# A reworked start: tile-wise gate steps, a fourth step in spare PSUM banks, and one transposing DMA per tile

## The chip, the cores and the metric

The kernel runs on one core of one Trainium2 chip. The metric is the device time of one execution in microseconds; 185.24 us is the median of three runs of the kernel before the change (185.03 to 185.57).

## What is computed

The input x is 2048 rows of 448. Each row is normalised; the normalised rows feed a gated network and a complex linear recurrence, and the two results are multiplied and added to x:

```
xn = layernorm(x)                                   # 2048 x 448
h[t] = Lam_bar * h[t-1] + B_bar @ xn[t]             # complex, 448 states
s = 2 * real(h @ C) + xn * Dskip
g = silu((sigmoid(xn @ w_gate) * (xn @ w_up)) @ w_down)     # inner width 1792
out = x + s * g
```

## The kernel before

**Tiling.** The 2048 rows are four chunks of 512, a chunk is four tiles of 128 rows. A chunk needs its normalised rows transposed: `xnT` holds seven slots of 512 columns. In slot s the partitions 0 to 63 hold features 64s to 64s+63 and the partitions 64 to 127 the next 64 features, round the end of the 448. TensorE uses it in two halves: lines 707 and 708 issue a pair of matmuls with 64 contracted rows each, one on the lower and one on the upper half of the array, and the two run beside each other. A step (`gu_step`) is one block m of 128 gate or up columns in both halves of the inner width: seven such pairs over the 512 columns of a chunk, into one of three two-bank PSUM tiles `gu`. `g0.3` is gate block 3 of chunk 0, `u0.0` up block 0. The gate result leaves PSUM through a Tanh on ScalarE (line 721), the up result through VectorE (line 724). Two further one-bank PSUM tiles, `acc`, are used in turn by the transposes, by `b_phase` and by the output matmuls.

**The head.** Chunk 0 is started by hand (lines 962 to 989). TensorE first runs matmuls on zeros (L418). The tiles 0 to 3 of x are loaded on the SP and ACT queues, the gate weights in three blocks for each half of the width (m 0 to 1, 2 to 3, 4 to 6), the lower half on SP and the upper on ACT. A tile goes through `stats` (L424, L425, VectorE), the square root on ScalarE (L450), a reciprocal (L452) and the normalisation (L469, VectorE). `pe_transpose` (L501 to 503) transposes it with eight TensorE operations, six over the full array and two of 64 columns, into an `acc` bank, and a copy brings it to `xnT` (tile 0 on ScalarE, L506; the others on VectorE, L509). `columns` (L540, L542) turns three small parameter rows into columns. The gate steps m 0 and 1 then take tiles 0 and 1 one at a time; after the transposes of tiles 2 and 3 come m 2 over two tiles, then m 0, 1 and 2 over tiles 2 and 3, and then the ordinary steps from `g0.3`.

**Later chunks.** `norm` runs on ScalarE (L474), POOL copies the first 64 features to the end of the 512-wide row buffer `xn` (L477), and `dma_transpose` issues two transposing DMAs a tile on SP (L375): one for the even slots and one for the odd. `skip_row` (L482) multiplies the same buffer by `dbc`, the broadcast Dskip. There are eight `xn` buffers.

**Order.** TensorE's order is that of the program text, VectorE's too while `pl.seq` is set. Everything else is ordered by a list scheduler (`Plan`) from the costs and transfer rates written in the code; it fixes the order before the run, and at run time each engine keeps it and waits for what it needs. DMAs issued on SP and ACT share eight completion semaphores in turn, so that the ninth waits for the landing of the first, and so on. SP issues in this order: x tile 0, three gate blocks, two up blocks (one for each half), x tiles 4 to 7 as one transfer, two up blocks, `dbc`, the B matrices (L375), the transposes of chunk 1.

Of the kernel before, what the change touches and what calls it, by code (L numbers as in the profile page):

```python
# [18 lines left out]
D = 448  # L19
F = 1792  # L20
P = 128
# [224 lines left out]
def kernel(  # L246
# [39 lines left out]
    NXN = 8  # L286
    xn = [sbt(f"xn{i}", [512]) for i in range(NXN)]
    xnT_raw = [sbt(f"xnT{i}", [7 * L]) for i in range(3)]
    xnT = [flat(t[:], 7, L) for t in xnT_raw]
    hF_raw = [sbt(f"hF{i}", [FT * L]) for i in range(2)]  # L290
# [69 lines left out]
    BLK = {"g": [(0, 2), (2, 4), (4, 7)], "u": [(0, 3), (3, 7)]}  # L360
# [25 lines left out]
    load_w("SP", "g", 0, 0, rate=90e3)  # L386
    load_w("SP", "g", 0, 1)
    load_x(1, 1, "ACT")
    load_x(2, 2, "ACT")
    load_w("ACT", "g", 1, 0, rate=90e3)  # L390
    load_w("SP", "g", 0, 2)
    load_w("ACT", "g", 1, 1)
    load_w("ACT", "g", 1, 2)
# [13 lines left out]
    for h in range(2):  # L407
        load_w("SP", "u", h, 0, rate=215e3)
    load_x(4, 4, rate=140e3)
    for h in range(2):  # L410
        load_w("SP", "u", h, 1, rate=260e3)
    load("SP", "dbc", P * D * 2, dbc[:], A_Dskip.unsqueeze(0).to_broadcast((P, D)))
# [53 lines left out]
    def norm(t):  # L466
        b = t % NXN
        if t < TPC:
            add("DVE", 0.42, lambda: V.tensor_scalar(out=xn[b][:, 0:448], in0=x_all[:, t, :],  # L469
                                                     scalar1=meanf[:, t, :], scalar2=rsd[:, t, :],  # L470
                                                     op0=ALU.subtract, op1=ALU.mult),
                r=[("x", t), ("mf", t), ("rs", t)], w=[("xn", b)])
        else:
# [3 lines left out]
            add("POOL", 0.2, lambda: G.tensor_copy(out=xn[b][:, 448:512], in_=xn[b][:, 0:64]),  # L477
# [6 lines left out]

    acc_n = [0]
# [9 lines left out]
    def pe_transpose(t):  # L495
        b, a, js = t % NXN, next_acc(), slice(t * P, t * P + P)
        tp = flat(acc[a][:].bitcast(BF16)[:, 0:7 * P], 7, P)

        def f():
            for s in range(6):  # L500
                T.transpose(tp[:, s, :], xn[b][:, s * H:s * H + P], ident[:, :])  # L501
            T.transpose(tp[0:H, 6, :], xn[b][:, 384:448], ident[:, :])
            T.transpose(tp[H:P, 6, :], xn[b][:, 0:H], ident[:, :])
        add("PE", 0.46, f, r=[("xn", b), "ident"], w=[("acc", a)])
        if t == 0:
# [6 lines left out]
    def dma_transpose(t):  # L512
        b, c = t % NXN, t // TPC
        js = slice((t % TPC) * P, (t % TPC) * P + P)
        k = ("xnT", c % 3, t % TPC)
        al = ["xnT2free"] if c == 2 else []
        tload([k + ("a",)], xnT[c % 3][:, 0:7:2, js], xn[b][:], P * 1024, r=[("xn", b), ("xnw", b)] + al)
        tload([k + ("b",)], xnT[c % 3][:, 1:6:2, js], xn[b][:, 64:448], P * 768, r=[("xn", b)] + al)
# [16 lines left out]
    def columns(a):  # L535
        vps = flat(gu[a][:, 0, 0:12], 4, 3)
# [6 lines left out]
        add("PE", 0.4, f, r=["ident"] + [("vrow", k) for k in range(3)], w=[("gu", a)])  # L543
        pv = sbt("pv", [3, 4], FP32)
        dt_b = C("dt", 4, BF16)
        add("DVE", 0.1, lambda: V.tensor_copy(out=pv[:].rearrange("p k i -> p i k"), in_=vps[:]), r=[("gu", a)], w=["pv"])
# [150 lines left out]
    SW = 0.1  # L697

    def gu_mm(c, k, m, a, lo, hi, first):
        x = xnT[c % 3]  # L700
        ts = slice(lo * P, hi * P)
# [3 lines left out]
        def f():  # L705
            for s in range(7):
                T.matmul(gu[a][:, 0, ts], lhsT=w_[0:H, s, ms], rhs=x[0:H, s, ts], start=(s == 0), stop=(s == 6))  # L707
                T.matmul(gu[a][:, 1, ts], lhsT=w_[H:P, (s + 1) % 7, ms], rhs=x[H:P, s, ts],  # L708
# [3 lines left out]
                   r=xr(c, lo, hi) + [("w", k, 0, m), ("w", k, 1, m)], w=[("gu", a)], name=f"{k}{c}.{m}")  # L712
# [3 lines left out]
    def gu_evac(c, k, m, a):  # L716
# [3 lines left out]
        if k == "g":  # L720
            add("ACT", act(1024), lambda: A.activation(th, gu[a][:], ACT.Tanh, scale=0.5),  # L721
                r=[("gu", a)], w=[tk])
        else:
            add("DVE", dve1(1024), lambda: V.scalar_tensor_tensor(out=ho, in0=th, scalar=1.0, in1=gu[a][:],  # L724
                                                                 op0=ALU.add, op1=ALU.mult),
                r=[("gu", a), tk], w=[hk])
# [23 lines left out]
    def b_phase(c, mid=None):  # L750
# [5 lines left out]
        rs = [(slice(0, H), 6), (slice(H, P), 5)]  # L756
# [210 lines left out]
    for t in (0, 1):  # L967
        chain(t, 1)
        norm(t)
# [125 lines left out]
```

## Time and profile before

| what | value |
|---|---|
| median of the runs shown | 185.24 us |
| the profiled execution: span from the first to the last instruction | 183.7 us |
| difference, what lies around the span | about 1.5 us |
| TensorE's granted clock over the span | 1.000 |
| first full-array transpose, tile 0 | 5.34 us after the start of the span |
| first gate pair | 7.89 us |
| `g0.3` starts | 13.87 us |
| `u0.0` starts | 19.91 us |

The profiled execution has a span; its own full time is not listed apart from the three runs, so the 1.5 us is taken against their median.

The trace also gives, for each DMA, the time from its issue to its landing. For the transfers of the head, in order of landing (sizes in KB of 1024 bytes; the last column adds the sizes up):

| transfer | queue | issued at, us | landed at, us | KB | KB so far |
|---|---|---|---|---|---|
| x tile 0 | SP | 0.7 | 3.1 | 112 | 112 |
| x tile 1 | ACT | 0.8 | 3.4 | 112 | 224 |
| x tiles 2, 3 | ACT | 1.2 | 5.1 | 224 | 448 |
| gate, lower, m 0-1 | SP | 1.2 | 7.08 | 224 | 672 |
| gate, upper, m 0-1 | ACT | 1.7 | 7.54 | 224 | 896 |
| gate, lower, m 2-3 | SP | 2.0 | 9.09 | 224 | 1120 |
| gate, upper, m 2-3 | ACT | 2.4 | 9.80 | 224 | 1344 |
| gate, lower, m 4-6 | SP | 2.6 | 11.16 | 336 | 1680 |
| gate, upper, m 4-6 | ACT | 3.2 | 12.26 | 336 | 2016 |
| up, lower, m 0-2 | SP | 7.1 | 14.21 | 336 | 2352 |
| up, upper, m 0-2 | SP | 7.7 | 15.82 | 336 | 2688 |
| x tiles 4-7 | SP | 8.4 | 19.04 | 448 | 3136 |
| up, lower, m 3-6 | SP | 9.1 | 20.88 | 448 | 3584 |
| up, upper, m 3-6 | SP | 9.8 | 22.48 | 448 | 4032 |
| dbc | SP | 11.2 | 22.66 | 112 | 4144 |

How to read the profile: an engine's share of the span says nothing of what sets the end; the chain of waits does. A stretch in which an engine's busy time equals the stretch cannot be shortened by an earlier arrival of its data, only by less work or by starting it earlier. The landing of a transfer is later than its issue by the queue ahead of it, and here that queue is most of it.

### The profile page before, as it was taken

The numbers are of one execution on the slowest core, as the hardware profiler recorded it, in microseconds if no ns is written. First come the engines' busy times: TensorE is split into PE (matmuls) and PEld (weight loads), VectorE is DVE, ScalarE is ACT, GpSimd is POOL, SyncE is SP. The second block draws the span as 40 slices with busy tenths as digits, with TensorE's granted clock in tenths as the row PEclk, the third lists the DMA queues.
The fourth block names the chain that finished last, engine by engine and source line by source line (L and its number), as shares of the span: only waits on it lengthen the run. The fifth ranks groups of instructions, "written<-read, shape, count | busy, mean of one in ns | idle before, by whom it ended". The sixth has DMA issues, their size and how long they took to land.

```text
span 183.7 us, 3601 instructions
## 1 busy us (share of the span) xinstructions
PE 177.4 (97%) x1402; PEld 90.4 (49%) x1402; DVE 166.4 (91%) x296; ACT 94.8 (52%) x152; POOL 34.2 (19%) x95
## 2 busy tenths in 40 slices
PE   7699999999999999999999999999999999999992
PEld 2585555465554444455554444444555444455551
DVE  3873899899999998999999999999999998999973
ACT  3689993958599978665310452367120445211100
POOL 7370465000048557700000000000000000000000
PEclk9999999999999999999999999999999999999999
DMA  5999994489801370243000000002000000001121
GB/s 137 255 225 223 155 166 90 90 256 266 231 0 26 74 82 21 50 82 71 0 2 0 29 0 0 4 0 75 0 4 0 25 25 5 25 0 52 57 73 50
DMA packets 30258, 13.44 MB, mean 73 GB/s; under 512 B 19744, under 2 KB 30240, under 8 KB 30240
## 3 DMA queue, kind: packets, MB, share of 16 engines
q1 hardware_dynamic: 28336, 12.05, 30.7%
q10 hardware_dynamic: 1808, 1.15, 2.5%
q8 instruction: 11, 0.18, 0.4%
q14 instruction: 7, 0.06, 0.1%
q0 software_dynamic: 96, 0.00, 0.0%
HBM read 6.77 MB, written 1.84 MB: 47 GB/s over the span
## 4 chain that ended last, share of the span: by engine, by line
PE 93%; DMA 3%; DVE 1%; issue 1%; POOL 1%; DVEq 0%; POOLq 0%
PE gu L707 45%; PE gu L903 14%; PE acc L932 11%; PE acc L903 9%; PE gu L775 8%; DMA hF<-in_A_Lambda_re_dram 3%; PE gu L708 2%; PE acc L778 2%; PE gu L761 2%; POOL hF L353 1%; PE acc L501 0%; DVE o_t L948 0%; PE acc L764 0%; DVE o_t L944 0%; DVE o_t L941 0%
## 5 line engine op out<-in xcount | busy, mean ns | idle before, releaser
L708 PE MATMUL gu<-xnT,wG 64*128 64x512 bf16 (+2 forms) x245 | 46.0, 333 | 0.0
L707 PE MATMUL gu<-xnT,wG 64*128 64x512 bf16 (+2 forms) x245 | 46.0, 333 | 0.0
L707 PE MATMUL gu<-xnT,wU 64*128 64x512 bf16 x196 | 45.8, 376 | 0.0
L708 PE MATMUL gu<-xnT,wU 64*128 64x512 bf16 x196 | 45.8, 376 | 0.0
L721 ACT ACTIVATE sig<-gu 128x1024 f32<-128x1024 f32 x21 | 21.3, 1021 | 22.0 <-PE gu L708 21.9
L903 PEld LDWEIGHTS <-hF 128*128 128x128 bf16 x224 | 21.9, 98 | 20.7 <-issue 0.2
L707 PEld LDWEIGHTS <-wG 64*128 64x128 bf16 x245 | 21.9, 94 | 18.7
L707 PEld LDWEIGHTS <-wU 64*128 64x128 bf16 x196 | 18.4, 94 | 22.1
L724 DVE SCALAR_TENSOR_TENSOR hF<-sig,gu 128x1024 bf16<-128x1024 f32 x21 | 25.5, 1216 | 2.9 <-PE gu L708 1.6
L903 PE MATMUL gu<-wd,hF 128*128 128x448 bf16 x140 | 27.9, 352 | 0.0
L842 DVE TENSOR_TENSOR_SCAN wv<-c_r,st,z 128x512 bf16<-128x512 f32 x18 | 22.9, 1276 | 0.0
L932 PE MATMUL acc<-cT,hT 128*128 128x448 bf16 (+1 forms) x112 | 22.6, 346 | 0.0
L708 PEld LDWEIGHTS <-wG 64*128 64x128 bf16 x245 | 21.8, 94 | 0.0
L909 ACT ACTIVATE g_t<-gu 128x448 bf16<-128x448 f32 x10 | 5.4, 541 | 29.2 <-DVE o_t L946 12.9
L708 PEld LDWEIGHTS <-wU 64*128 64x128 bf16 x196 | 18.4, 94 | 0.0
L789 ACT CAST bus<-gu 128x1024 bf16<-128x1024 f32 x12 | 11.9, 1011 | 12.4 <-PE gu L761 12.2
L903 PE MATMUL acc<-wd,hF 128*128 128x448 bf16 x84 | 16.9, 352 | 0.0
L775 PE MATMUL gu<-xnT,bT 128*128 128x512 bf16 x72 | 16.7, 379 | 0.0
L932 PEld LDWEIGHTS <-hT 128*128 128x128 bf16 x119 | 11.5, 98 | 10.1 <-issue 0.4
L424 DVE BATCH_NORM_STATS2 bst<-x_all 128x6 f32<-128x448 bf16 x12 | 7.0, 610 | 5.7 <-DMA x_all<-in_A_x_dram 5.7
L795 ACT CAST bus<-acc 64x256 bf16<-64x256 f32 (+1 forms) x24 | 8.8, 369 | 6.4 <-PE acc L778 6.1
L944 DVE TENSOR_TENSOR o_t<-acc,xd 128x448 bf16<-128x448 f32 (+1 forms) x16 | 9.6, 601 | 1.3 <-PE acc L932 1.2
(138 smaller groups left out, 240.1 us busy)
## 6 DMA issues: line engine op xcount, KB each, us to landing
out_dram<-o_t SPq DMA_DIRECT2D x15, 112.0 KB, 1.7
wd<-in_B_w_down_dram SPq DMA_DIRECT2D x2, 784.0 KB, 5.5
x_all<-in_A_x_dram SPq DMA_DIRECT2D x3, 448.0 KB, 4.5
wU<-in_B_w_up_dram SPq DMA_DIRECT2D x2, 448.0 KB, 12.2
wU<-in_B_w_up_dram SPq DMA_DIRECT2D x2, 336.0 KB, 7.6
wG<-in_B_w_gate_dram SPq DMA_DIRECT2D x2, 224.0 KB, 6.5
wG<-in_B_w_gate_dram ACTq DMA_DIRECT2D x2, 224.0 KB, 6.6
xnT<-xn SPq DMA_TRANSPOSE x24, 2.4
```

The lines of the kernel that those rows point to most:

```text
L424: add("DVE", 0.6, lambda: V.bn_stats(out=bst[b][:], in_=x_all[:, t, :]), r=[("x", t)], w=[("bst", b)])
L707: T.matmul(gu[a][:, 0, ts], lhsT=w_[0:H, s, ms], rhs=x[0:H, s, ts], start=(s == 0), stop=(s == 6))
L708: T.matmul(gu[a][:, 1, ts], lhsT=w_[H:P, (s + 1) % 7, ms], rhs=x[H:P, s, ts], start=(s == 0), stop=(s == 6))
L721: add("ACT", act(1024), lambda: A.activation(th, gu[a][:], ACT.Tanh, scale=0.5), r=[("gu", a)], w=[tk])
L724: add("DVE", dve1(1024), lambda: V.scalar_tensor_tensor(out=ho, in0=th, scalar=1.0, in1=gu[a][:], op0=ALU.add, op1=ALU.mult), r=[("gu", a) ...
L775: T.matmul(gu[slots[pt]][:, i, :], lhsT=bT[:, kt, i, pt * P:pt * P + P], rhs=x[:, 2 * kt, :], start=(first and kt == 0), stop=(not first a ...
L789: add("ACT", act(1024), lambda: A.copy(out=bus[u][:], in_=gu[slots[pt]][:]), r=key(pt), w=[("bus", u)])
L795: add("ACT", 0.3, lambda ns=ns, d=d, q=q, l=l, i=i: A.copy(out=bus[u][d, l, ns], in_=acc[a3[i]][q, 0:256]), r=[("acc", a3[i])] + ([("bus", ...
L842: dve(1.194, lambda k=k: V.tensor_tensor_scan(out=wv[:, k, :], data0=rb, data1=z[:, k, :], initial=(st[pt][:, k, :] if c else 0.0), op0=AL ...
L903: T.matmul(d, lhsT=hF[c % 2][:, m, h, js], rhs=wd[:, ft, :], start=(ft == 0), stop=(ft == FT - 1))
L932: T.matmul(y, lhsT=hT[c % 2][:, hm, js], rhs=cT[:, cm, c0:c1], start=(i == 0 and not on_pe), stop=(i == 6))
L944: add("DVE", dve1(n), lambda od=od, y=y, c0=c0, c1=c1: V.tensor_tensor(out=od, in0=y, in1=xq[:, c0:c1], op=ALU.add), r=[key, ("xd", q)], w ...
```

## The change

It touches the head of chunk 0 and the way a later tile is transposed.

- **Loads.** x tiles 0 and 2 go on SP, 1 and 3 on ACT, each as a transfer of its own. The gate weights go in two blocks a half (m 0 to 2, m 3 to 6). The upper-half up blocks are issued on ACT, after the square roots of tiles 1 and 2. On SP the transposing DMA of tile 3 comes next, then x tiles 4 to 7, the two lower-half up blocks and `dbc`.
- **The row buffer.** `xn` is 896 wide and holds the row twice, and there are four buffers, not eight. In the head a VectorE copy of 64 features follows the normalisation of tiles 0 to 2; tile 3 is written twice over by one wider normalisation. In later chunks POOL copies all 448 features.
- **Transposes.** Seven full-array TensorE transposes for each of the tiles 0, 1 and 2, with tile 2's copy to `xnT` on ScalarE; tile 3 goes by DMA. A later tile takes one transposing DMA over 896 columns. The slots of `xnT` are permuted to fit (`SL`).
- **Gate steps.** m 0, 1 and 2 take tiles 0, 1 and 2 one at a time. Block m 3 runs over tiles 0 to 2 at once in the two `acc` banks. Then m 0, 1, 2 and 3 take tile 3. The ordinary steps start at `g0.4`. `columns` uses an `acc` bank.

The diff, cut to its core:

```diff
-    NXN = 8
-    xn = [sbt(f"xn{i}", [512]) for i in range(NXN)]
+    NXN = 4
+    xn = [sbt(f"xn{i}", [2 * D]) for i in range(NXN)]
+    SL = [4 * s % 7 for s in range(7)]
...
-    BLK = {"g": [(0, 2), (2, 4), (4, 7)], "u": [(0, 3), (3, 7)]}
+    BLK = {"g": [(0, 3), (3, 7)], "u": [(0, 3), (3, 7)]}
...
     load_x(0, 1, "SP")
-    load_w("SP", "g", 0, 0, rate=90e3)
-    load_w("SP", "g", 0, 1)
     load_x(1, 1, "ACT")
-    load_x(2, 2, "ACT")
-    load_w("ACT", "g", 1, 0, rate=90e3)
-    load_w("SP", "g", 0, 2)
-    load_w("ACT", "g", 1, 1)
-    load_w("ACT", "g", 1, 2)
+    load_x(2, 1, "SP", rate=140e3)
+    load_x(3, 1, "ACT", rate=140e3)
+    load_w("SP", "g", 0, 0, rate=115e3)
+    load_w("ACT", "g", 1, 0, rate=115e3)
+    load_w("SP", "g", 0, 1, rate=145e3)
+    load_w("ACT", "g", 1, 1, rate=145e3)
...
-    for h in range(2):
-        load_w("SP", "u", h, 0, rate=215e3)
-    load_x(4, 4, rate=140e3)
-    for h in range(2):
-        load_w("SP", "u", h, 1, rate=260e3)
-    load("SP", "dbc", P * D * 2, dbc[:], A_Dskip.unsqueeze(0).to_broadcast((P, D)))
...
+            n = 2 if t == 3 else 1
+            add("DVE", 0.3 * n, lambda: V.tensor_scalar(out=flat(xn[b][:, 0:n * D], n, D), in0=bcast_mid(x_all[:, t, :], n),
...
+            if n == 1:
+                add("DVE", 0.1, lambda: V.tensor_copy(out=xn[b][:, D:D + H], in_=xn[b][:, 0:H]),
+                    r=[("xn", b)], w=[("xnw", b)])
...
-            add("POOL", 0.2, lambda: G.tensor_copy(out=xn[b][:, 448:512], in_=xn[b][:, 0:64]),
+            add("POOL", 0.5, lambda: G.tensor_copy(out=xn[b][:, D:2 * D], in_=xn[b][:, 0:D]),
...
-            for s in range(6):
-                T.transpose(tp[:, s, :], xn[b][:, s * H:s * H + P], ident[:, :])
-            T.transpose(tp[0:H, 6, :], xn[b][:, 384:448], ident[:, :])
-            T.transpose(tp[H:P, 6, :], xn[b][:, 0:H], ident[:, :])
+            for k in range(7):
+                lo = k * P if k < 4 else H + (k - 4) * P
+                T.transpose(tp[:, k, :], xn[b][:, lo:lo + P], ident[:, :])
...
-        tload([k + ("a",)], xnT[c % 3][:, 0:7:2, js], xn[b][:], P * 1024, r=[("xn", b), ("xnw", b)] + al)
-        tload([k + ("b",)], xnT[c % 3][:, 1:6:2, js], xn[b][:, 64:448], P * 768, r=[("xn", b)] + al)
+        tload([k + ("a",), k + ("b",)], xnT[c % 3][:, :, js], xn[b][:], P * 1792, r=[("xn", b), ("xnw", b)] + al)
...
     stats(0)
     stats(1)
-    for t in (0, 1):
-        chain(t, 1)
-        norm(t)
+    head_norm(0)
+    head_norm(1)
+    load_w("ACT", "u", 1, 0, rate=145e3, r=[("sd", 1)])
     stats(2)
-    stats(3)
     slots0 = [next_gu() for _ in range(3)]
     pe_transpose(0)
     pe_transpose(1)
-    columns(slots0[2])
-    for t in (2, 3):
-        chain(t, 1)
-        norm(t)
-    for j in range(2):
-        for m in range(2):
-            gu_mm(0, "g", m, slots0[m], j, j + 1, not (j or m))
+    head_norm(2)
+    load_w("ACT", "u", 1, 1, rate=145e3, r=[("sd", 2)])
+    stats(3)
+    head_steps(0, True)
+    columns(1)
     pe_transpose(2)
-    pe_transpose(3)
+    head_steps(1, True)
+    head_norm(3)
+    dma_transpose(3)
+    load_x(4, 4, "SP", rate=145e3)
+    load_w("SP", "u", 0, 0, rate=200e3)
+    load_w("SP", "u", 0, 1, rate=217e3)
+    load("SP", "dbc", P * D * 2, dbc[:], A_Dskip.unsqueeze(0).to_broadcast((P, D)))
     silu_table()
     pl.seq = False
-    gu_mm(0, "g", 2, slots0[2], 0, 2, True)
+    head_steps(2, False)
+    gu_mm(0, "g", 3, None, 0, 3, False)
     for m in range(3):
-        gu_mm(0, "g", m, slots0[m], 2, 4, False)
+        gu_mm(0, "g", m, slots0[m], 3, 4, False)
         gu_evac(0, "g", m, slots0[m])
+    gu_mm(0, "g", 3, None, 3, 4, False)
+    gu_evac(0, "g", 3, None)
...
-    for i in range(3, 13):
+    for i in range(4, 13):
         gu_step(0, i)
```

Here `head_norm(t)` is `chain(t, 1)` and `norm(t)`, and `head_steps(t, first)` runs `gu_mm` for m 0, 1 and 2 over tile t. With no `gu` tile given, `gu_mm` writes the two `acc` banks and `gu_evac` empties them with two Tanh operations of 512 columns.

## The prediction

> **What bounds the kernel now.** I read the page's shares first, then the stretches, to see where TensorE (PE) has no slack, then its waits, and last the landings of the head's transfers (table above).
>
> ```profile
> PE 177.4 (97%) x1402; PEld 90.4 (49%) x1402; DVE 166.4 (91%) x296; ACT 94.8 (52%) x152; POOL 34.2 (19%) x95
> PE 93%; DMA 3%; DVE 1%; issue 1%; POOL 1%; DVEq 0%; POOLq 0%
> ```
>
> ```profile
> core 0: us, PE busy (x) PEld busy (x) DVE busy (x) ACT busy (x) POOL busy (x), PEclk, DMA share, GB/s
> ...
> 6.60:7.60 1.00, 0.04 (x2) 0.00 (x1) 0.96 (x4) 0.79 (x3) 0.37 (x2) 1.00 1.06 230
> ...
> 13.90:180.10 166.20, 166.19 (x1246) 82.42 (x1240) 156.28 (x268) 86.38 (x140) 25.94 (x65) 1.00 0.29 63
> 180.10:183.70 3.60, 0.00 (x0) 0.00 (x0) 0.80 (x3) 0.00 (x0) 0.00 (x0) 1.00 0.11 32
> ```
>
> From 13.9 us to 180.1 us PE is busy in 166.19 of 166.20 us, at the full clock; then comes a tail of 3.6 us. The change leaves that work as it is. So the whole question is when PE gets past the head, and whether a new hole opens behind it. My mark is the start of `g0.4`, by which the same gate work is done in both kernels. Now: `g0.3` starts at 13.87 and has seven pairs 0.215 us apart, so `g0.4` starts at **15.38**. The hole at 6.6 to 7.6 ends with PE's only DMA wait:
>
> ```profile
> PE gu L540 <- DMA hF<-in_A_Lambda_re_dram: 1.0, 1, 1.0
> PE acc L501 <- DVE xn L469: 0.5, 1, 0.5
> ```
>
> The parameter row landed at 7.49, but the first gate block's upper half landed at 7.54: two arrivals end that hole together, and moving one alone gains little.
>
> **PE's own work in the head.** Rows used (starts in PE's timeline): a pair of 64x128 matmuls every 0.056 us (28 of them from 7.89 to 9.41), of 64x256 every 0.110 (28 from 10.79 to 13.87), of 512 every 0.215; a tile's transposes 0.62 from tile to tile (9.56, 10.18), of which a full-array one takes 0.058 and each change to or from the half-array form about 0.15; `columns` 0.26. From 7.63 to 15.38 PE spends 0.26 + 1.57 + 0.09 + 1.23 + 3.08 + 1.51 = 7.74.
>
> After, from the first gate pair at X: tile 0 takes 21 x 0.056 = 1.18; `columns` with a switch 0.41; tile 2's transposes 7 x 0.058 + 0.15 = 0.56; tiles 1 and 2 2.36; m 3 over 384 columns, between the 256 and 512 rows, 7 x 0.163 = 1.14. That is X + 5.65. Then tile 3: 28 x 0.056 = 1.57, about 0.1 more after a wait. With no wait `g0.4` starts at X + 7.22: PE's own work shrinks by about half a microsecond. The rest is arrivals.
>
> **X, the first gate pair.** Two bounds. Below, by the row: norm 0 starts at 4.89 and takes 0.40; the new copy of 64 columns behind it costs about 0.1 to 0.18 (the reciprocal and `pv` rows, 0.13 to 0.18); seven transposes and the ScalarE copy (0.91) end near 7.05. Above, the weights: m 0 to 2 of both halves now lie behind four x tiles, 448 + 672 = 1120 KB, where m 0 to 1 needed 896 KB and landed at 7.54. Between 896 KB (7.54) and 2016 KB (12.26) landings came at 237 KB/us, so 224 KB more is 0.95 us: **X = 8.5**. I take the weights. Block m 3 to 6 completes the same 2016 KB, at 12.26, before X + 4.5 = 13.0 when PE asks for it.
>
> **Tile 3 by DMA.** Its place in VectorE's fixed order sets the issue:
>
> ```profile
> 5.46 0.40 DVE L469 TENSOR_SCALAR xn<-x_all,meanf,rsd 128x448 bf16<-128x448 bf16 x1
> 5.78 0.62 DVE L424 BATCH_NORM_STATS2 bst<-x_all 128x6 f32<-128x448 bf16 x1
> ...
> 7.26 0.59 DVE L509 COPY xnT<-acc 128x896 bf16<-128x896 bf16 x1
> ...
> 8.92 0.40 DVE L469 TENSOR_SCALAR xn<-x_all,meanf,rsd 128x448 bf16<-128x448 bf16 x1
> ```
>
> VectorE is nearly full from 3.15 to 9.3. The change adds three copies (about 0.4 in all) and doubles norm 3's width (0.40 to some 0.65), and it puts tile 2's norm and the `pv` copy ahead of norm 3. Walking the new order with these durations: norm 1 and its copy end at 6.2, stats 2 at 7.0, tile 1's copy at 7.6, norm 2 with its copy at 8.45, stats 3 at 9.25, the square root at 9.55, norm 3 at 10.5 (10.7 if `pv` waits for `columns` at X + 1.6). SP issues the transpose at about 10.6.
>
> ```profile
> xnT<-xn SPq DMA_TRANSPOSE x24, 2.4
> ```
>
> The eight of chunk 1 took 2.4 to 3.8 us to land, each half of a tile and with the queues almost empty. So the lower bound is 10.6 + 2.4 = 13.0. But now 224 KB must pass beside the up blocks, which the change issues on ACT from about 5.1 and 7.4. By the table of landings: 2016 KB of x and gate weights plus these 224 KB land at 13.7 if nothing of the up weights goes first; with the first ACT up block ahead (336 KB more, 2576) at 15.2; with both (3024) at 18.2. The bounds are 13.0 and 18.2. I take **15.3**: the SP queue drains with the gate weights, some 1.5 us before the transpose's data can start, and the ACT queue has that time and then its share. PE wants tile 3 at X + 5.65 = 14.15, so it waits about 1.15 us, and `g0.4` starts at 15.3 + 0.1 + 1.57 = 16.97, **1.6 us later** than now. In TensorE's order nothing can fill that hole: `g0.4` is behind tile 3.
>
> [...] This trace has 0.62 us for a whole tile on PE against 2.4 us and more to land half a tile. [...]
>
> **Behind the waiting transpose on SP** stand x tiles 4 to 7, the two lower up blocks, `dbc`, the B matrices. They were issued from 7.1 on; now none leaves before about 11.9. `u0.0` needs the lower up block 0, now behind 2016 + 224 + 448 + 784 + 336 = 3808 KB (before: 2688 KB, at 15.82, with 4.1 us to spare). From 3584 KB (20.88) and 4032 KB (22.48) that reads as 21.7; at the two-queue rate of 237 KB/us from 12.26 on, 19.8. `u0.0` is due 3 x 1.51 = 4.53 after `g0.4`: at 21.5 in my case, so this costs 0 to 0.2 there, but in a case without the transpose's delay it alone gives away any gain beyond 19.91 - 19.8 = 0.1.
>
> [...] The rows agree that a second queue adds little (237 GB/s at 9 to 11 us with two queues at work, 223 at 17 to 19 with one); taken strictly, it sets 21.7 rather than 19.8.
>
> **Costed at nothing.** Later tiles: one DMA for two saves some 1.3 us of SP's issue a tile (eight took 10.9 us from 25.2 to 36.2), but PE does not wait for them now (last landing 37.30, asked for at about 39). POOL's copy grows from 0.24 to about 0.57 (between the 64- and the 192-column rows, carried on), POOL being 19% busy. Four buffers: norm 4 to 7 must now wait for skip rows 0 to 3, which need `dbc`, about 1.1 us later (224 KB at 197 KB/us). One skip row (0.39) fits in each 1.51 us up step beside the 1.2 us evacuation: the fourth by 28.5, its norm, copy and transpose (0.7 + 0.6 + 3.3) by 33.5, still before 37.3. Without that cover chunk 1 would start late, by up to as much. The B matrices landed at 27.9 and are due at 30.5, so they take 1.1 us more as well. The ScalarE copy of tile 2 (0.91) ends near X + 3.2, as tile 1's steps end (X + 3.3).
>
> **Rivals.**
> - *The transpose is not late.* It lands by 14.15 because it gets its share at once. Then X sets the time: 8.5 + 7.22 = 15.7, 0.3 later, and `u0.0` at 20.25 is near its weights: 185.3 to 185.9, say 185.5.
> - *Faster: the gate block lands early.* If rows of 768 and 1024 bytes move better than those of 512, X falls to its lower bound, 7.1. PE is ready for tile 3 at 12.75, the transpose at 13.0 gives 14.65, 0.7 earlier: **184.5**. It decides once tile 3 lands before 13.1 and the lower up block before 19.2. For it: PE's work is 0.5 less. Against it: 268 GB/s at 5 to 7 us with 512-byte rows and 237 at 9 to 11 with 768.
> - *Both up blocks go first.* Tile 3 at 17 to 18.2: 3.3 to 4.5 later, 188.5 to 189.7.
> - *It does nothing*, since PE is full anyway: only if all arrivals shift alike; it is inside the first rival.
>
> **The numbers.** 183.7 + 1.6 = 185.3 of span, with the same 1.5 around it; on the median 185.24 + 1.6 = 186.8. Chances: the forecast 0.54 (185.9 to 188.2), not late 0.20 (0.16 of it within 0.3%), faster 0.18, both blocks first 0.08. A measurement here tells 0.3%, 0.56 us, from no change. Faster 0.18, same 0.16, slower 0.66. The range reaches from the faster rival, 184.4, to 188.2.
>
> **What would show it.** Right: PE idle once, for about a microsecond, before the tile-3 steps, ended by the transposing DMA; first gate pair near 8.5; `g0.4` near 17.0; PE full from there on. Wrong: tile 3 lands before PE asks for it; the first gate pair starts at 7.1; or the hole is at `u0.0`, ended by the up weights, or at chunk 1.

## The result, and the profile after

The changed kernel takes 190.28 us (median of four runs, 189.01 to 190.69) against 185.26 us for the kernel before on the same chip: ratio 1.025, 95% interval 1.021 to 1.029. It is slower, as forecast, but by 5.0 us where 1.6 were forecast, and outside the range (184.4 to 188.2). The ratios here and below compare the executions within 1.5% of their kernel's fastest, the medians take in all of them, and the profiles of e2, e4 and e5 below come from slower ones, of which only the head is read. The profiled execution took 189.01 us, span 187.2 against 183.7. The page, as before:

```profile
PE 179.1 (96%) x1454; PEld 92.3 (49%) x1461; DVE 167.6 (90%) x297; ACT 96.3 (51%) x154; POOL 41.5 (22%) x95
```

TensorE is busy 1.7 us longer than before (179.1 against 177.4), though its order asks for less work. The stretches of the changed kernel show where (columns: stretch, its length, busy time of each engine, granted TensorE clock, DMA share, GB/s):

```profile
core 0: us, PE busy (x) PEld busy (x) DVE busy (x) ACT busy (x) POOL busy (x), PEclk, DMA share, GB/s
...
7.30:8.90 1.60, 0.24 (x3) 0.11 (x5) 1.42 (x6) 0.04 (x1) 0.00 (x0) 1.00 1.13 257
...
10.02:13.44 3.42, 3.42 (x59) 3.04 (x55) 0.75 (x3) 1.96 (x2) 2.16 (x7) 0.50 1.13 200
...
15.80:16.80 1.00, 0.20 (x6) 0.01 (x2) 1.00 (x4) 1.00 (x3) 0.00 (x0) 1.00 1.16 326
...
18.50:183.30 164.80, 164.37 (x1223) 81.68 (x1227) 156.43 (x264) 86.08 (x139) 33.40 (x65) 1.00 0.27 59
183.30:187.20 3.90, 0.00 (x0) 0.00 (x0) 0.74 (x3) 0.00 (x0) 0.00 (x0) 1.00 0.11 32
```

Read from the bottom. `g0.4` starts at 18.46 and TensorE ends at 183.24, 164.78 later; before it was 15.38 to 180.09, 164.71. So behind `g0.4` nothing was lost, the tail took 0.4 more (4.0 against 3.6), and 3.08 us were lost in the head. There, TensorE idles at 7.3 to 8.9, runs at **half clock** from 10.02 to 13.44 (only 59 matmuls in 3.42 us), and idles again at 15.8 to 16.8. TensorE's waits in the head name both idle stretches:

```profile
PE gu L705 <- DMA wG<-in_B_w_gate_dram: 1.4, 1, 1.4
PE gu L704 <- DMA xnT<-xn: 0.8, 1, 0.8
```

and the chain of work (start, length, what) shows how they hang together:

```profile
1.67 7.14 DMA wG<-in_B_w_gate_dram
...
8.86 0.23 PE gu L705
...
10.25 0.17 PE acc L537 x3
10.42 0.16 PE acc L539 x2
10.61 0.18 DVE pv L543
...
10.95 0.52 DVE xn L464
11.49 5.25 DMA xnT<-xn
...
16.78 0.21 PE gu L704
```

The upper gate block lands at 8.81; tile 0's steps; `columns`; VectorE's `pv` copy and, behind it, norm 3; the transposing DMA of tile 3, issued at 11.49 and landed 5.25 us later; then the tile-3 steps and `g0.4`. The two up blocks on ACT's queue, issued at 4.69 and 7.02, landed 8.5 and 8.9 us later, at 13.21 and 15.95, both ahead of the transpose:

```profile
4.69 0.60 ACTq L354 DMA_DIRECT2D wU<-in_B_w_up_dram  x1
7.02 0.60 ACTq L354 DMA_DIRECT2D wU<-in_B_w_up_dram  x1
...
wU<-in_B_w_up_dram ACTq DMA_DIRECT2D x1, 448.0 KB, 8.9
...
wU<-in_B_w_up_dram ACTq DMA_DIRECT2D x1, 336.0 KB, 8.5
```

This chain looks like the whole answer. The runs show that it is the longest of four of nearly one length.

### The profile page after: what moved, and what is told of

Read it like the earlier page. It is cut to its first block, busy times and chain, and to the rows that moved or that the text cites. A ratio compares the mean times of both kernels' runs of the same rounds, so it can differ in the third digit from the quotient of the medians.

```text
span 187.2 us, 3710 instructions
## 1 busy us (share of the span) xinstructions
PE 179.1 (96%) x1454; PEld 92.3 (49%) x1461; DVE 167.6 (90%) x297; ACT 96.3 (51%) x154; POOL 41.5 (22%) x95
## 4 chain that ended last, share of the span: by engine, by line
PE 89%; DMA 7%; DVE 1%; issue 0%; ACTq 0%; ACT 0%; DVEq 0%
PE gu L704 41%; PE gu L904 14%; PE acc L933 11%; PE acc L904 8%; PE gu L776 8%; DMA wG<-in_B_w_gate_dram 4%; DMA xnT<-xn 3%; PE gu L705 2%; PE gu L762 2%; PE acc L779 2%; DVE o_t L949 0%; DVE xn L464 0%; ACTq L354 0%; PE acc L765 0%; ACT L382 0%
## 5 line engine op out<-in xcount | busy, mean ns | idle before, releaser
L722 ACT ACTIVATE sig<-gu 128x1024 f32<-128x1024 f32 x21 | 21.4, 1022 | 23.4 <-PE gu L705 23.3
L704 PEld LDWEIGHTS <-wG 64*128 64x128 bf16 x280 | 23.8, 98 | 19.0 <-DMA wG<-in_B_w_gate_dram 0.6
L725 DVE SCALAR_TENSOR_TENSOR hF<-sig,gu 128x1024 bf16<-128x1024 f32 x21 | 25.5, 1212 | 1.6 <-PE gu L705 1.4
L705 PEld LDWEIGHTS <-wG 64*128 64x128 bf16 x280 | 23.7, 98 | 2.6 <-DMA wG<-in_B_w_gate_dram 1.5
L475 POOL COPY xn<-xn 128x448 bf16<-128x448 bf16 x12 | 9.8, 823 | 26.7 <-ACT xn L472 26.5
L776 PE MATMUL gu<-xnT,bT 128*128 128x512 bf16 x65 | 15.3, 379 | 0.4
L472 ACT ACTIVATE xn<-x_all,nmr,rsd 128x448 bf16<-128x448 bf16 x12 | 8.8, 756 | 4.6 <-DVE xd L480 3.5
```

Of the source, the lines that this page charges most:

```text
L472: add("ACT", 0.65, lambda: A.activation(xn[b][:, 0:448], x_all[:, t, :], ACT.Identity, bias=nmr[:, t, :], scale=rsd[:, t, :]), r=[("x", t) ...
L475: add("POOL", 0.5, lambda: G.tensor_copy(out=xn[b][:, D:2 * D], in_=xn[b][:, 0:D]), r=[("xn", b)], w=[("xnw", b)])
L704: T.matmul(bank[0][:, ts], lhsT=w_[0:H, s, ms], rhs=x[0:H, SL[s], ts], start=(s == 0), stop=(s == 6))
L705: T.matmul(bank[1][:, ts], lhsT=w_[H:P, (s + 1) % 7, ms], rhs=x[H:P, SL[s], ts], start=(s == 0), stop=(s == 6))
L776: T.matmul(gu[slots[pt]][:, i, :], lhsT=bT[:, kt, i, pt * P:pt * P + P], rhs=x[:, kt, :], start=(first and kt == 0), stop=(not first and k ...
```

## The experiments

Ratios are to the kernel before, run on the same chip, with the 95% interval. X is the start of the first complete gate pair. "Fetch" is the first 16 KB packet, within the span, of the queue that the profile calls instruction, and "matmul 223" TensorE's matmul number 223 in the profile, behind which some kernels stop.

| run | median us | ratio | X | half clock | tile 3 issued, landed | fetch ends | matmul 223 reached, goes on | `g0.4` |
|---|---|---|---|---|---|---|---|---|
| before | 185.26 | 1 | 7.89 | none | (PE) | 16.38 | 20.56, no stop | 15.38 |
| after | 190.28 | 1.025 | 8.86 | 10.02-13.44 | 11.49, 16.74 | 15.01 | 18.03, no stop | 18.46 |
| e1 | 189.53 | 1.020 | 8.47 | 8.46-11.87 | 12.13, 17.01 | 15.30 | 18.30, no stop | 18.85 |
| e3 | 188.17 | 1.013 | 8.48 | 7.74-14.56 | 12.14, 15.49 | 13.80 | 17.93, no stop | 18.89 |
| e4 | 189.0 | 1.016 | 8.86 | 18.01-21.43 | 11.41, 17.52 | 15.83 | 18.98, no stop | 20.12 |
| e6 | 188.94 | 1.016 | 8.77 | 8.88-12.29 | (PE) | 15.29 | 17.40, no stop | 19.11 |
| e7 | 188.46 | 1.015 | 8.92 | none | (PE) | 15.81 | 15.84, **17.31** | 18.05 |
| e8 | 190.49 | 1.026 | 9.26 | 9.32-12.74 | 10.28, 16.81 | 17.04 | 18.10, **18.63** | 18.92 |
| e10 | 186.18 | 1.005 | 8.85 | none | (PE) | 12.13 | 15.56, no stop | 16.39 |
| e11 | 186.64 | 1.008 | 8.81 | none | 10.29, 13.60 | 11.89 | 15.09, no stop | 15.75 |
| e13 | 189.31 | 1.019 | 7.9 | 18.04-21.45 | (PE) | 16.11 | 15.39, **17.69** | 17.87 |
| e14 | 187.68 | 1.011 | 7.08 | none | (PE) | 15.32 | 15.41, **16.87** | 16.94 |
| e17 | 185.87 | 1.005 | 7.24 | none | (PE) | 11.96 | 15.57, no stop | 15.79 |

**e1, the changed kernel again**, no edit.

> The changed kernel once more, nothing edited: a second profile beside the first, because its three timed runs were 1.2 to 1.7 us above the profiled one. Theory A (tile 3's transposing DMA ends the head): wherever the span is longer than 187.2, the DMA of tile 3 lands later than 16.74 by the same amount, PE waits longer for it, and the ordinary steps start later than 18.46. Theory B (TensorE's clock): the granted clock stays at half for two windows of 3.4 us instead of one, and PE has no longer wait. Theory C (something behind the head): the ordinary steps start at 18.5 as before and the difference lies after them.

189.53 us, 1.020 (1.011 to 1.030). The same picture with its parts shifted: half clock earlier, the transpose issued 0.64 later (12.13) and landed at 17.01. The head's order of events is stable, its times move by some tenths.

### Is it the transposing DMA?

**e2, tile 3 by TensorE** (`dma_transpose(3)` replaced by `pe_transpose(3)`), and **e5, the same with useless matmuls in the first hole**.

```diff
-    dma_transpose(3)
+    pe_transpose(3)
```

> One part undone: tile 3 is transposed by seven TensorE transposes and a VectorE copy, as tiles 0 to 2 are, instead of by the DMA. Theory A (the DMA of tile 3 is the cause and the whole of it): ordinary steps from about 16.5, some 2 us earlier than in the changed kernel, time near 187. Theory B (the late gate block and the half clock that follows are a second path, nearly as long): PE was ready for tile 3 at 15.8 in the changed kernel anyway, so only 1.0 us of waiting goes and 0.6 to 0.9 us of transposes comes: ordinary steps at 18.1 to 18.4, time 0 to 0.4 us better than the changed kernel.

> Both edits of the two runs before it: tile 3 on TensorE and TensorE kept busy for the gate block. If the DMA of tile 3 and the half clock are two paths of nearly the same length, neither edit alone gains 0.5 us but both together gain about 1.7: ordinary steps at 16.7, which is the gate block's landing (8.8) plus PE's own work (7.2 + 0.6); time about 186.7, still 1.3 to 1.5 over the kernel before. If one of them alone is the cause, this run equals the better of the two before it.

e2 191.96 us, 1.031 (1.023 to 1.039), e5 190.97 us, 1.018 (1.008 to 1.027), against 1.025 (1.021 to 1.029) of the change: no gain that can be told. They aren't clean. With no transpose to wait for, SP issued x tiles 4 to 7 and the lower up blocks at 3.2 to 4.8, among the gate blocks (the upper gate block landed at 10.07 in e2), and ScalarE, blocked at the issue of its own up blocks until a gate block had landed, copied tile 0 late (in e2 it issued at 8.01 and copied at 8.65). Both show a stop of 3.6 to 3.9 us behind matmul 223 for which the profile names no semaphore (18.66 to 22.54 and 17.14 to 20.77); I return to it.

**e3, no up blocks beside the transpose**: ScalarE's two are issued on SP behind it.

```diff
-    load_w("ACT", "u", 1, 0, rate=145e3, r=[("sd", 1)])
-    load_w("ACT", "u", 1, 1, rate=145e3, r=[("sd", 2)])
...
     dma_transpose(3)
     load_x(4, 4, "SP", rate=145e3)
-    load_w("SP", "u", 0, 0, rate=200e3)
-    load_w("SP", "u", 0, 1, rate=217e3)
+    for b in range(2):
+        for h in range(2):
+            load_w("SP", "u", h, b, rate=217e3)
```

> The changed kernel with the two upper-half up blocks taken off the ACT queue and put on SP behind tile 3's transposing DMA, so that nothing but the last gate block is in flight beside it. Theory A1 (the DMA is late because the up blocks on ACT go through the same engines beside it): it lands 2.4 to 3.3 us after its issue, near 14.5 instead of 16.7 to 17.0; PE is then ready for tile 3 later than that (15.3 to 15.8) and does not wait; ordinary steps at 17.0 to 17.4, 1.3 us earlier; but the last up block for u0.0 now comes near 22, so that up to 0.8 us may be lost again there. Theory A2 (a transposing DMA of 224 KB is that slow by itself): it still takes about 5 us and lands near 16.5, and the time is that of the changed kernel or worse.

188.17 us, 1.013 (1.009 to 1.017). The transposes' rows (by the tile `xnT`), of the changed kernel and of e3:

```profile
who waited for it (us, times):
  PE gu L704: 0.8, 1
...
DMA to landing us min/median/max: 5.2/5.2/5.2
```

```profile
who waited for it (us, times):
...
DMA to landing us min/median/max: 3.3/3.3/3.3
```

The landing falls from 5.2 to 3.3 us, and nobody waits for it. But `g0.4` of the profiled execution is no earlier (18.89): half clock lasted two windows (7.74 to 14.56), and behind the tile-3 steps TensorE waited 0.5 us for ScalarE's first Tanh (L722). The ten executions of e3 go with the mean granted clock: three at 0.997 to 1.000 took 186.6 to 187.2 us, four at 0.988 to 0.991 took 188.0 to 188.5, and three at 0.982, the profiled one among them, 188.7 to 189.5. By these clocks the same kernel does or doesn't fall to half clock, for one window or two.

**e8, an earlier issue**: the column matmuls ahead of the first gate steps, so that `pv` and norm 3 don't wait for them.

```diff
+    columns(1)
     head_steps(0, True)
-    columns(1)
```

> The changed kernel with the parameter columns ahead of the first gate steps on TensorE, not behind them: VectorE's copy of them, which stands ahead of tile 3's norm in its order, then no longer waits for the gate block. Both theories expect the transposing DMA to be issued at about 10.2 instead of 11.5 to 12.1. Theory A1 (it ends when the up blocks on ACT have gone through): it still lands at 16 to 16.7, time within 0.4 us of the changed kernel. Theory A3 (the late issue is the cause): it lands 1.2 us earlier, near 15.5, ordinary steps near 17.2, time 1.2 us better.

190.49 us, 1.026 (1.018 to 1.035), like the change itself. Issued 1.2 us earlier (10.28), the transpose landed at the same time (16.81):

```profile
DMA to landing us min/median/max: 6.5/6.5/6.5
```

So its landing is not set by its place in VectorE's order. It goes with the second up block on ACT's queue, which landed at 15.95 in the changed kernel, 16.21 in e1, 15.90 in e8 and 16.75 in e4: each time the transpose landed 0.8 to 0.9 us behind it.

### The half clock

**e6, tile 3 by TensorE with SP's order kept**: a 2 KB stand-in DMA that reads norm 3's output takes the transpose's place on SP. **e7, the same with 10 useless matmuls of zeros** ahead of the first gate steps. **e4, the changed kernel with these 10**.

```diff
-    dma_transpose(3)
...
+    add("SP", 1.2, lambda: Q.dma_start(out=stand[0:16, :], in_=xn[3][0:16, D:D + H]), ...)
...
+    add("PE", 0.0, turn3, ...)
+    add("DVE", 0.64, lambda: V.tensor_copy(out=xnT[0][:, :, 3 * P:4 * P], in_=tp3[:, :, :]), ...)
```

> Tile 3 on TensorE as in e2, but a DMA of 2 KB that reads the end of tile 3's row buffer stands in the place of the transposing one on SP, so that x tiles 4 to 7 and the up blocks are issued when the changed kernel issues them, in the same order, and every other engine keeps its order but for one VectorE copy. Theory A (the transposing DMA's wait decides, the half clock and the gate block are a second path up to 1 us shorter): PE's wait of 1.0 to 1.7 us is gone, 0.6 to 0.9 us of transposes come in, ordinary steps at 17.5 to 18.0, time 0.5 to 1.0 us under the changed kernel, near 188.8. Theory D (the up weights, not tile 3, are what the queue makes late): ordinary steps earlier, but a hole opens at u0.0 and the time is that of the changed kernel.

> e6 with the ten matmuls on zeros of e4 in the wait for the gate block. Theory A: with the DMA of tile 3 gone and the clock kept at 1.0, only the gate block's landing (8.4 to 8.9) and PE's own work (7.2 + 0.6) are left: ordinary steps at 16.5, time near 186.7, 1.3 over the kernel before. If the half clock costs nothing once tile 3 is on TensorE, this run equals e6.

> The changed kernel with ten more matmuls on zeros (512 columns, 2.1 us) on TensorE between the transposes of tile 1 and the first gate pair, where it stood idle for the gate block. Both theories expect the granted clock to stay at 1.0. Theory A: the DMA of tile 3 still lands near 16.6, PE only waits longer for it (2.7 us instead of 1.0), ordinary steps at 18.3, time within 0.3 us of the changed kernel. Theory B (the half clock alone is the cause): ordinary steps 1.5 us earlier, near 16.9.

e6 188.94 us, 1.016 (1.007 to 1.025); e7 188.46 us, 1.015 (1.009 to 1.022); e4 189.0 us, 1.016 (1.008 to 1.023). One and the same stretch, of e6 and then of e7, whose two later rows belong to the next part:

```profile
8.88:12.29 3.41, 3.41 (x55) 2.99 (x55) 0.95 (x5) 0.30 (x1) 0.65 (x2) 0.50 1.12 207
```

```profile
8.88:12.29 3.41, 3.41 (x98) 3.03 (x98) 1.00 (x5) 1.50 (x3) 1.43 (x3) 1.00 1.13 207
14.50:15.80 1.30, 1.30 (x38) 1.04 (x35) 1.29 (x4) 1.30 (x4) 1.22 (x3) 1.00 1.09 305
16.10:17.25 1.15, 0.00 (x0) 0.00 (x0) 1.15 (x3) 1.15 (x3) 0.00 (x0) 1.00 1.12 207
```

With the hole filled the clock stays at 1.00 and TensorE does 98 matmuls where it did 55. The tile-3 steps start at 15.06 instead of 16.34. In e4, too, the clock stays full through the head, and TensorE is ready for tile 3 at 14.40, 5.54 behind X (the prediction had 5.65); but the transpose lands at 17.52, and the wait of 3.0 us is followed by half clock (18.01 to 21.43). In e6 another wait stands behind it:

```profile
PE gu L704 <- ACT hF L722: 1.0, 1, 1.0
```

The first Tanh, which frees the first `gu` bank for `g0.4`, starts only at 18.07: the list scheduler had put a table load (1.28 us) and six operations of the tables (L572, L579, L581) ahead of it. ScalarE works through them without a break, but begins late: it first stands 2.83 us for tile 2's transposes, which TensorE runs behind the first gate steps and `columns`.

```profile
12.34 0.91 ACT L504 COPY xnT<-acc 128x896 bf16<-128x896 bf16 x1 [2.83 <-PE acc L501]
...
18.07 3.80 ACT L722 ACTIVATE hF<-gu 128x1024 bf16<-128x1024 f32 x4
```

In the changed kernel this wall stands right behind the transpose. ScalarE's rows there, ahead of the first Tanh and from it on:

```profile
16.67 0.61 ACT L581 ACTIVATE spm<-hT 128x512 bf16<-128x512 f32 x1
17.39 3.82 ACT L722 ACTIVATE hF<-gu 128x1024 bf16<-128x1024 f32 x4
```

`g0.4` follows the start of that Tanh by 1.04 to 1.07 us in the changed kernel, e1, e3 and e6. In the changed kernel the Tanh could have started at about 17.2 to 17.3 at the earliest, so `g0.4` at about 18.3 (an estimate from these rows): in this execution an earlier landing alone would have gained 0.1 to 0.2 us.

### The stop without a semaphore

In e7 TensorE issues nothing from 15.84 to 17.31 (the row 16.10 to 17.25 has no matmul). Its profile names no releaser, but one packet of the instruction queue was on its way from 14.51 to 15.81. The two longer stops of e2 and e5 have such a packet too (ends 21.18 and 18.72), and all three are behind matmul 223.

**e10 and e11, all four walls taken away together** (the wait for the transpose, the half clock, the tables ahead of the first Tanh, the fetch): `columns` first, between 5 and 3 useless matmuls; all up blocks on SP, behind norm 3; the tables' Abs and Sin behind the first three Tanh; tile 3 by TensorE (e10) or by DMA (e11).

> All the found walls taken away together, tile 3 by TensorE: the column matmuls ahead of the first gate steps with useless matmuls of zeros (5 before, 3 after) in the hole, both up blocks of ScalarE's queue on SP in the order of the kernel before, a 2 KB stand-in in the place of tile 3's transposing DMA, and the tables' Abs and Sin held behind the first three Tanh. Theory of several walls: first gate pair at 8.4 to 8.9, granted clock 1.0 through the head, the tile-3 steps from about 14.3, g0.4 at 16.0 to 16.5, time 186 to 186.6. Rival (instruction fetch of TensorE): a hole of 1 us or more with no semaphore behind it after the fetch's packet, g0.4 at 17.3 or later, time 187.5 or more. Rival (nothing but the transposing DMA matters): no better than the run with tile 3 by TensorE and filled, 188.5.

> The same with tile 3 by its transposing DMA. Theory: issued at about 10.3 with nothing of the up blocks beside it, landed 2.4 to 3.4 us later, 12.7 to 13.7, so ahead of TensorE's need at 13.5 to 14.3; granted clock 1.0; g0.4 at 15.7 to 16.3; 185.5 to 186.3 us. Rival (instruction fetch): a hole without a semaphore, g0.4 at 17 or later, 187 or more. Rival (the DMA lands late for a reason of its own, such as its small packets): landing at 15 or later and the wait for it still there.

e10 186.18 us, 1.005 (1.002 to 1.007); e11 186.64 us, 1.008 (1.005 to 1.010). Four of the five microseconds are back, with the change's x and gate loads, tile-wise steps, fourth step in accumulator banks and seven transposes all in place. These edits were made together, so what each is worth beside the others isn't shown. In e11 the transpose, issued at 10.29, landed 3.3 us later, at 13.60, 0.5 us before the tile-3 steps (14.08), and `g0.4` began at 15.75.

e10, with no waits left in the head, is TensorE's own work from X. e11 gives back 1.5 us between 24 and 33 us; 0.7 of it are waits for VectorE's evacuations (L725), for the rest the profile names no releaser.

**e13, the gate blocks of the kernel before in e10** (three a queue, x tiles 2 and 3 in one load, up blocks directly behind them on SP, no stand-in, m 2 over tiles 0 and 1 at once, 3 useless matmuls). **e14, the same without useless matmuls and with `columns` behind the first four steps**.

```diff
-    BLK = {"g": [(0, 3), (3, 7)], "u": [(0, 3), (3, 7)]}
+    BLK = {"g": [(0, 2), (2, 4), (4, 7)], "u": [(0, 3), (3, 7)]}
...
```

> The last open term, the start X of the first gate pair: the loads of the kernel before (three gate blocks a queue, both up blocks on SP right behind them), and everything else as in the run with the walls taken away and tile 3 by TensorE: columns first behind 3 useless matmuls, tile-wise steps (third block's two tiles together), fourth step in accumulator banks, seven transposes a tile, tables behind the first Tanh. If the two large gate blocks were what was left of the loss (X 8.85 there, 7.9 before): first pair at 7.6 to 7.9, g0.4 1.0 earlier than there, 15.2 to 15.5, time 185.1 to 185.5, the same as before. Rival (the loss of 0.9 us sits elsewhere, in the tile-wise order itself or in contention of the up blocks that now run beside the head): g0.4 at 16 or later, 186 or more.

> The same without the useless matmuls and with the column matmuls behind the first four gate steps instead of ahead of them, so that the first pair waits only for tile 0's copy (about 7.0) and the first gate blocks (7.0 to 7.3) and not for the parameters. Theory: first pair at 7.1 to 7.4, g0.4 at 14.8 to 15.2, time 184.7 to 185.2, a little faster than before. Rival (a wall behind it: the tables' chain, the first Tanh, or TensorE's instruction fetch, takes it back): g0.4 at 15.4 or later although the first pair came earlier, 185.3 or more.

e13 189.31 us, 1.019 (1.014 to 1.024); e14 187.68 us, 1.011 (1.008 to 1.014). Both expectations missed: X came 0.9 and 1.8 earlier, and the time got worse. Both stop behind matmul 223, for 2.3 and 1.5 us. In e13 half clock follows:

```profile
14.62:18.03 3.41, 1.33 (x44) 1.09 (x40) 2.19 (x5) 2.85 (x3) 0.23 (x1) 1.00 1.12 223
18.04:21.45 3.41, 3.41 (x18) 1.24 (x16) 2.82 (x10) 0.52 (x1) 1.09 (x3) 0.50 1.35 144
```

**e15, the up blocks behind the fetch's request**, and **e16, with tile 2's copy on VectorE as well**.

> The run before it (three gate blocks, columns behind the first four steps) lost 1.46 us at 15.41, at TensorE's matmul 223, while a 16 KB instruction fetch was still on its way (13.93 to 15.32, beside the up blocks that SP had issued at 6.6 to 9.9). Here the up blocks, x tiles 4 to 7 and the skip row are issued behind norm 3, at about 10.3, so after TensorE asks for the fetch (at about matmul 95, 9.7). If the fetch waits behind the up blocks' packets: packet at about 10 to 12, no hole at matmul 223, g0.4 at 15.4 to 15.7 where it was 16.9, time 185.2 to 185.8. Rival (the hole is no matter of the fetch, but of the tile-wise steps' form at that place): the hole of 1.4 us stays at 15.4 and the time at 187.7.

> The same, and tile 2's copy out of the accumulator on VectorE instead of ScalarE, whose copy there waited behind its 1.28 us table load (10.70; TensorE idle 0.9 us from 10.74 to 11.65). Theory: that hole falls to 0 to 0.3 us, g0.4 at 14.6 to 15.2, a little ahead of the 15.38 of the kernel before, time 184.6 to 185.2. Rival: VectorE's copy (0.6 us) delays norm 3 by as much, tile 3 comes 0.6 later and the hole moves there, or the up blocks, issued 3 us later than in the kernel before, are late at the second block's first step: 185.3 or more.

e15 187.09 us, 1.006 (1.002 to 1.010); e16 186.73 us, 1.006 (1.002 to 1.009). The edit missed its aim: the reason given to the scheduler made no wait, and SP issued the up blocks at 6.7 and 6.3 as before. e15 is thus e14 again, with the stop (15.40 to 17.36); e16 has it too (15.11 to 16.39). They don't test what a quieter queue does for the fetch.

**e17 and e18, the same two with a real wait**: the 2 KB stand-in, which reads norm 3's output, ahead of the up blocks on SP.

```diff
     head_norm(3)
+    stand = sbt("stand", [H])
+    add("SP", 1.2, lambda: Q.dma_start(out=stand[0:16, :], in_=xn[3][0:16, D:D + H]), ...)
     for h in range(2):
         load_w("SP", "u", h, 0, rate=215e3, r=[("xn", 3)])
```

> The run before the last again, with the edit that it lacked: SP issued the up blocks at 6.7 there too, since the reason given to the planner orders work but makes no wait. Now a 2 KB stand-in, which reads norm 3's output, is issued ahead of the up blocks on SP, so that they start at about 10.9. If the instruction fetch waits behind the up blocks' packets: the packet ends at 11 to 13 instead of 15.3 to 15.8, no hole at matmul 223 (1.4 to 2.0 us there), g0.4 at 15.4 to 15.8, time 185.4 to 185.9. Rival (the hole has to do with the matmuls' form at that place): the hole stays, 187.

> The same with tile 2's copy on VectorE. There TensorE's holes were 0.66 us ahead of tile 3's transposes and 1.28 us at matmul 223. Theory: the second goes, g0.4 at 15.0 to 15.3, time 184.8 to 185.4, the same as before or a little faster. Rival: the up blocks, issued 4 us later than there, come late at the first up step or at its second block (a hole of TensorE at 19 to 25): 185.5 or more.

e17 185.87 us, 1.005 (1.002 to 1.007); e18 186.48 us, 1.006 (1.005 to 1.008). The stretch of the fetch, the queue's own line in it, and the stretch behind matmul 223, first in e14:

```profile
13.93:15.32 1.39, 1.39 (x53) 1.36 (x49) 1.39 (x4) 0.89 (x2) 0.22 (x1) 1.00 1.12 284
15.62:16.80 1.18, 0.01 (x1) 0.00 (x0) 0.70 (x3) 1.18 (x2) 0.23 (x1) 1.00 1.12 211
```

```profile
q1 hardware_dynamic: 444, 0.40, 104.8%
q8 instruction: 1, 0.02, 5.8%
```

then in e17:

```profile
10.68:11.96 1.28, 1.28 (x26) 0.93 (x22) 0.06 (x1) 1.27 (x3) 0.94 (x5) 1.00 0.06 12
15.40:16.80 1.40, 1.40 (x26) 0.88 (x22) 1.10 (x3) 1.40 (x3) 0.22 (x1) 1.00 1.09 218
```

```profile
q10 hardware_dynamic: 30, 0.02, 5.8%
q8 instruction: 1, 0.02, 5.7%
```

In e14 the fetch shares the engines with 444 packets of queue q1, which then carries an up block and x tiles 4 to 7, and TensorE does nothing from 15.62 to 16.80. In e17 the queues are nearly empty (12 GB/s) when it passes, 3.3 us earlier, and TensorE works through. In all eight kernels that stop behind matmul 223 (e2, e5, e7, e8, e13 to e16) TensorE goes on 1.4 to 2.1 us after the packet's end, which lies between 15.0 and 21.2; in the other twelve profiles the packet ended 2.1 us or more before matmul 223, and none stops. So the stop is the fetch's. e18 misses: its fetch is as early and its `g0.4` (15.65) too, but it loses 0.6 us at 30 to 32 us, where the profile names no releaser.

### What costs nothing, and what doesn't beat the kernel before

**e9, the later tiles alone** (the head of the kernel before; one transposing DMA a tile, four 896-wide buffers, POOL's copy of 448 columns). **e12, with seven full-array transposes for tiles 2 and 3**, a 64-column VectorE copy ahead of each.

> The later tiles alone: head of the kernel before (its loads, its gate order, its transposes), with the changed kernel's one transposing DMA a tile, 896-wide xn with four buffers, the POOL copy of 448 columns and the turned column order. My theory (the whole loss of the change lies in the head; matmul time after g0.4 was 164.8 us in both kernels): the same as before, 185.3 us plus or minus 0.3, first chunk and TensorE's end as in the profile before (g0.4 near 15.4, end near 180.1). Rival: half the xn buffers or the POOL copy (0.82 us a tile where 0.57 was estimated) delays tiles in later chunks: a hole ahead of some chunk's first gate matmul and 0.5 us or more lost.

> A candidate to beat both: the head of the kernel before, the later tiles of the changed one, and tiles 2 and 3 turned by seven full-array transposes instead of eight, with a 64-column copy on VectorE ahead of them. A transpose takes about 0.07 us, so TensorE saves 2 x 0.07 = 0.14 us if the copies (0.18 us each on VectorE) lie beside other work: 184.9 to 185.3. Rival: VectorE's copies delay tile 2 and tile 3 by 0.2 us each where TensorE waits for them: 185.3 to 185.7.

e9 185.86 us, 1.002 (1.0003 to 1.0039): 0.4 us, 0.05 to 0.7, slower. Its TensorE row ends at 180.24 (180.09 before) and has one hole that the kernel before had not, 0.3 us at 31.07, where L761 (`b_phase`) waits for VectorE's evacuation L724; e12 has the same at 32.62, while the changed kernel, e10 and e17 have none there:

```profile
13.80:180.20 166.40, 166.10 (x1244) 82.30 (x1238) 157.35 (x268) 86.36 (x140) 32.22 (x65) 1.00 0.31 62
```

e12 185.42 us, 1.002 (0.9996 to 1.0038): no difference that can be told. None of these runs beat the kernel before.

## Why the prediction was right or wrong, point by point

- **"PE is full, so only the start of `g0.4` matters; later tiles and `u0.0` cost nothing."** Right. 164.78 against 164.71 us behind `g0.4`; the lower up block landed at 19.81, before its step (22.99). POOL's copy took 0.82 us, not 0.57, without effect. But e9 allows the later tiles up to 0.7 us, where nothing was put, and its trace has the hole of 0.3.
- **X = 8.5 by the weights.** Right: 8.86, ended by the upper gate block (8.81). The rival at 7.1 is out. But the price put on it was wrong: the idle time from 6.6 to X costs not only itself: the clock behind it was 0.50 from 10.02 to 13.44.
- **PE's own work, X + 5.65 to tile 3.** The count is right: in e4 it took 5.54, and in e11, where `columns` lies ahead of X, 5.27 us were left. In the changed kernel it took 6.96 (8.86 to 15.82), because one clock window at half speed followed the idle time. I had taken the rows of the kernel before at full clock, and hadn't asked what a longer hole does to the rows behind it.
- **The issue at 10.6.** It came at 11.49; norm 3 waited for `pv`, as the step said it might, and `columns` came later. e8 shows that it didn't matter.
- **The landing at 15.3: a step that failed.** I let the ACT queue have 1.5 us and then its share, so that one up block went first. The runs show both blocks landing first and the transpose behind the second, at 16.7 to 17.0 in the changed kernel, e1 and e8, however early it is issued (10.3 to 12.1); without them it took 3.3 us. The rival "both up blocks go first" was the mechanism. I had put 0.08 on it, at 17 to 18.2; it came at 16.74, since the bytes moved faster than my table (18.2 by it). Along the chain 1.44 of the 1.9 us between the forecast span (185.3) and the measured one lie in this step, 0.4 in the tail. (By the table 2240 KB land at 13.6, not at 13.7 as I read; nothing hangs on it.)
- **"`g0.4` starts at the landing + 0.1 + 1.57", with PE idle once: the other step that failed.** It was true as a picture and wrong as a cause: I looked for the one arrival that ends last, and with the landing at 15.3 this sum would have failed too. Three more walls, which no step named, stood near it. Half clock: from X to the tile-3 steps it cost 1.4 us (6.96 against 5.54 in e4; 7.57 in e6 against 6.14 in e7). The tables ahead of the first Tanh: `g0.4` not before about 18.3 in the changed kernel, 18.9 and 19.1 in e3 and e6. The instruction fetch: nothing behind matmul 223 before 16.4 to 17.1, by its end at 15.01 and the 1.4 to 2.1 us behind it; the changed kernel came there at 18.03, so there it cost nothing yet. Taking away the transpose alone therefore gained 1.3 us (e6), and all four 4.1 (e10).
- **The median** was a further 1.3 us above the profiled execution. Its other executions had spans of 188.4 to 188.9 at nearly the same mean clock (0.989 to 0.991), so the number of half-clock windows doesn't explain it. This is left open.
- **What is left** of e10 and e17 against the kernel before, 0.9 and 0.7 us, is mostly in their `g0.4`, 1.0 and 0.4 later, and in e10 that is X. Whether the later tiles cost something in these two, as e9's hole suggests, stays open: in e17, as in the changed kernel, the time behind `g0.4` is that of before (164.7).

## What to carry to other kernels

When a profile shows one wait at the end of a start-up phase, ask what would be late next if it were gone, and test by taking away all candidates together: here no single one gained more than about 2 us of 5. Price an idle stretch of TensorE with the clock that may follow it (0.50 for 3.41 us here), and transfers by all the bytes on every queue ahead of them (the transpose took 5.2 us here and 3.3 in e3), instruction fetches included (the packet ended at 15.32 in e14 and at 11.96 in e17). The steps made of more, smaller matmuls also came sooner to the place where the fetch must have ended: matmul 223 at 20.56 before and at 18.03 after, although the head is longer.

## What the runs showed of the hardware

- **The granted clock changed in windows of 3.41 us**, one after the other: every recorded stretch of one clock but the last is a whole number of times 3.413 us long (174.08 us, 51 times, in the changed kernel). Idle time of TensorE within one window and the next window's clock, over the twenty profiles (before, after and eighteen runs), from the first recorded window on: 1.57 us (e3) and more was followed by half clock each time (after 1.76, e1 1.71, e6 1.89, e8 2.01, e13 2.08), 1.43 and less at full clock never; between, 1.46 was (e12) and 1.55 wasn't (e15). One window already at half clock was followed by another with 0.74 idle (e3). The kernel before stands at 1.40 (4.15 to 7.56). The profiled execution of e12 took 187.29 us where its others took 185.1 to 185.9. In these runs half clock thus followed from about 1.5 us of idle time within a window on (an estimate from these rows).
- **TensorE's instructions come in 16 KB packets**, one for about 126 matmuls with their weight loads (ten packets over 1259 matmuls in e10). With the queues nearly empty the first began near matmul 95 (e3, e10, e11, e17, e18: 87 to 100), so it is probably asked for there (an estimate from these starts), and the eight kernels that stop do so behind 223. In these five it ended 1.1 to 1.5 us after matmul 95, in the other fifteen profiles, with weight loads on the queues, 2.6 to 7.3. In e13, e14 and e16 it was a stop of 1.3 to 2.3 us.
- **A transposing DMA beside two up blocks** on the other queue took 4.9 to 6.5 us (e1, the changed kernel, e4, e8) where it took 3.3 without them (e3, e11).
